# Gating h of the first MoE straight out of the PSUM banks it is computed in

## The chip, the cores and the metric

The program runs on one core of a Trainium2 chip. Its engines are TensorE (PE in the rows; PEld are its weight loads), VectorE (DVE), ScalarE (ACT), GpSimd (POOL) and SyncE (SP), each with its own queue that it works off strictly in order; they meet through semaphores. [...] The metric is the device time of one execution in microseconds, as the median of several. The profile is of one execution.

## The reference

```
X   = fft(fft(x, axis=1), axis=2).real          # x: 8 x 3072 x 256, fp32
h   = X @ w_in                                   # 24576 tokens, 256 -> 2048
g   = h * clip(h + 3, 0, 6) / 6
y   = g @ w_out                                  # 2048 -> 256
e   = argmax(y @ w_gate);  p = softmax(y @ w_gate)[e]       # one of 8 experts a token
out = p * relu(y @ w1[e]) @ w2[e]                # 256 -> 1024 -> 256; out: 24576 x 256
```

## The kernel before, in words

Every fp32 product is made of three TensorE products in the fp32r type (high part by high, high by low, low by high), so each operand of a matmul is kept as a high part (a ScalarE copy that rounds) and a low part (operand minus high part).

The first phase, some 2090 us of the span, does the transform and the first MoE. A *step* (`step(s)`, 384 of them) takes 512 tokens and 256 of the 2048 columns of h. Eight steps (`STEPS`) make a *chunk* of tokens, 48 steps a batch. One step consists of:

- `mm1`: 14 matmuls of 256 columns into a tile `ab` of two PSUM banks, A in the first and B in the second.
- `h_of`: ScalarE copies A to SBUF (tile `A`), and VectorE forms h for tokens k and for the mirrored tokens: `h[0] = A - B` and `h[1] = A + B`, each 128x512.
- the gates: `relu6` on ScalarE gives r = relu(h/6 + 1/2) for both halves; `gate_h` on VectorE puts min(r, 1)*h in r's place; ScalarE copies it to `gh` (the high part), and GpSimd subtracts, `gl = r - gh`.
- `mm2` of the step three before (`LAG`): 16 matmuls of 264 columns with `gh` and 8 with `gl` into four accumulator banks `acc`, over the eight steps of a chunk.

The tiles `ab` come from a pool of two (four banks); the four `acc` banks are the other half of PSUM. A piece of the transform (`fft_g0`, `fft_g12`: 13 to 28 matmuls, tiles `fe`, `fo`, `f`) takes a tile of the same pool of two; there is one piece in each chunk, at the step in which the accumulators of the chunk before are read out too. That step also begins the routing of the finished chunk (`routing`: small VectorE and GpSimd work, four indirect DMAs from GpSimd's queue), and its rank product rides in the free half of the transform's tile. In the other steps VectorE also folds the input of the next batch: one operation, now and then two, on the SBUF tiles `R` and `H` (516 or 774 elements a partition), after a step's gates.

In the kernel before the gates of step s are written in step s+1 and read h from an SBUF tile `h` (two buffers a half). The order on each engine is not the order of the code: a scheduler sorts the instructions by priority and by its own model of when a buffer is free, and the pools decide how many steps may be under way. An instruction marked `keep_in_program_order` is left where the code has it; that mark is on the folds, not on matmuls.

The second phase, some 1260 us, runs the experts on tiles of 512 or 256 routed tokens. No line of it changes.

Of the lines that matter:

```
BUFS = dict(h=2, r=4, gh=4, gl=4)                                    # before
ab_ps = ps1.enter_context(tc.tile_pool(name="ab_ps", bufs=2, space=PSUM))
```

Of the kernel before, what the change touches and what calls it, by code (L numbers as in the profile page):

```python
# [10 lines left out]
F32 = mybir.dt.float32  # L11
# [5 lines left out]
AF = mybir.ActivationFunctionType  # L17
# [9 lines left out]
GW = 264  # L27
# [16 lines left out]
EC = 5  # L44
EX = 6
RKW = 4
BUFS = dict(h=2, r=4, gh=4, gl=4)
EXTRA = 23
LATE = (0, 0, 1, 1, 2, 3, 3, 4, 5, 5, 6, 6, 7, 7, 8, 8, 8, 9)
RK = 2  # L50
# [24 lines left out]
def tile_fft_moe(ctx, tc, xr, xf, xcoef, w_in, w_out, w_gate, w1, w2, tabs, fm, misc, tri, sgn8, dstc, maskc, out):  # L75
# [24 lines left out]
    tiles, hold = {}, {}  # L100
# [21 lines left out]
    def wo(i, f):  # L122
        if (i, f // 8) not in WOh:
            WOh[i, f // 8] = pc.tile([P, 8, GW], F32R, tag=f"WO{i}{f // 8}", name=f"WO{i}{f // 8}")
        return WOh[i, f // 8][:, f % 8]
# [20 lines left out]
    dve, act, pool, pe, sp = nc.vector, nc.scalar, nc.gpsimd, nc.tensor, nc.sync  # L146
# [6 lines left out]
    def ab_tile(name):  # L153
        hold["last"] = t = ab_ps.tile([P, 2, 512], F32, tag="ab", name=name)
        return t


    def bank(name):
        if "hp" in hold:
            return hold["hp"].tile([P, 512], F32, tag="hp", name=name)  # L160
        return ab_tile(name)[:, 1]

    def mm_group(dst, terms):
        for n, (l, r) in enumerate(terms):
            pe.matmul(dst, l, r, start=(n == 0), stop=(n == len(terms) - 1))  # L165

    def pinned(i):
        if hold.get("fold"):
# [11 lines left out]
    def add(eng, o, a, b):  # L180
        pinned(eng.tensor_tensor(out=o, in0=a, in1=b, op=ALU.add))  # L181

    def sub(eng, o, a, b):
        i = eng.tensor_tensor(out=o, in0=a, in1=b, op=ALU.subtract)  # L184
        pinned(i)
        return i
# [79 lines left out]
    def xterm(b, c0, n):  # L266
        return [(XN[:, c0:c0 + P], sgn_of[b][:, 0:n])]

    def fft_g0(b, pq):
        def e_mm(st):  # L270
            ab = st["ab"] = ab_tile(f"fe{b}_0")
            mm_group(ab[:, 0, 0:258], fft_terms(SC0, 0, 0, "c", 0) + xterm(b, X_T0, 258))
            mm_group(ab[:, 1, 0:256], fft_terms(SC0, 1, 0, "c", 1))

        def e_ev(st):
            ab = st["ab"]
            v = lambda i: pq[:, i].rearrange("p (a c) -> p a c", a=2)
            act.activation(v(0), ab[:, :, 0:256], AF.Copy)
            dve.tensor_copy(pex[:, b:b + 1], ab[:, 0, 256:257])
            dve.tensor_tensor(out=v(1), in0=ab[:, :, 0:256], in1=v(0), op=ALU.subtract)  # L280

        def o_mm(st):
            ab = st["ab2"] = ab_tile(f"fo{b}_0")
            for i, n, c0 in ((0, 258, X_T0 + P), (1, 256, X_T1)):
                full = fft_terms(SS0, 1 - i, 0, "s", i) + xterm(b, c0, n)
                edge = fft_terms(SC0, i, P, "c", i, 1)
                for t, (l, r) in enumerate(full[:1] + edge + full[1:]):
                    rows = slice(0, 1 if 0 < t <= len(edge) else P)
                    pe.matmul(ab[rows, i, 0:n], l, r, start=t == 0, stop=t == len(full + edge) - 1)

        def o_ev(st):
            ab = st["ab2"]
            v = lambda i: pq[:, i].rearrange("p (a c) -> p a c", a=2)
            act.activation(v(2), ab[:, :, 0:256], AF.Copy)
            dve.tensor_copy(qex[:, b:b + 1], ab[:, 0, 256:257])
            dve.tensor_tensor(out=v(3), in0=ab[:, :, 0:256], in1=v(2), op=ALU.subtract)

        return [(e_mm, e_ev), (o_mm, o_ev)]
# [191 lines left out]
        for i in range(2):  # L490
            mm_group(ab[:, 1, i * 256:(i + 1) * 256], [(WB[a][:, f[i]], pq[:, 2 + c, c0:c0 + 256]) for a, c in PASS])

    def h_of(ab, h, s):
        A = pw.tile([P, 2, 256], F32, tag="Ac", bufs=AB, name=f"A{s}")
        v = [ab[:, n].rearrange("p (i n) -> p i n", i=2) for n in range(2)]
        act.activation(A, v[0], AF.Copy)  # L496
        sub(dve, h[0], A, v[1])
        add(dve, h[1], A, v[1])

    def relu6(r, h):  # L500
        act.activation(r, h, AF.Relu, bias=half, scale=1.0 / 6.0)  # L501
# [2 lines left out]
    def halves(tag, dt, s):  # L504
        return [pw.tile([P, 2, 256], dt, tag=tag, bufs=BUFS[tag], name=f"{tag}{s}_{n}") for n in range(2)]

    def gate_h(g, r, h):
        dve.scalar_tensor_tensor(out=g, in0=r, scalar=1.0, in1=h, op0=ALU.min, op1=ALU.mult)  # L508

    def mm2(acc, gh, gl, f0, first, last, mid=(), ntau=4):  # L510
        def one(i, t, g, w, st, sp_):
            lhs = g[t // 2][:, i, (t % 2) * P:(t % 2 + 1) * P]
            pe.matmul(acc[t][:, 0:GW], lhs, wo(w, f0 + i), start=st, stop=sp_)  # L513
        for i in range(2):
            for t in range(ntau):
                one(i, t, gh, 0, first and i == 0, False)
                one(i, t, gh, 1, False, False)
            if i == 0:
                for f in mid:
                    f()  # L520
        if last:
            for t in range(ntau):
                for i in range(2):
                    one(i, t, gl, 0, False, i == 1)
        else:
            for i in range(2):
                for t in range(ntau):
                    one(i, t, gl, 0, False, False)
# [78 lines left out]
    if True:  # L607
# [52 lines left out]
        NS = len(chunks) * STEPS  # L660
# [257 lines left out]
        def plan_early():  # L918
            e0 = 8 * (NCH - EC) + 18 + RKW - 3
            fill[e0].append(lambda: None)  # L920
            pfill[e0].append(early_mm)
            fill[e0].append(early_pick)
            fill[e0 + 4].append(lambda: (first_sets(), load_x(0), load_w(0), load_x(1)))
            for n in range(4):
                fill[e0 + 6 + EG * n].append(lambda n=n: in_order(prep_w(0, lambda n: dve)[n]))
            fill[e0 + 10 + EX].append(lambda: prep_x(0))

        def step(s):
            z = s - LAG
            if s < NS:  # L930
                b, g, c = chunks[s // STEPS]
                f0 = 2 * (s % STEPS)
                ab = ab_tile(f"ab{s}")
                mm1(ab, f0, gt[(b, g)], c * 256, q3[s // STEPS % 2])
            hold["ride"] = None
            for f in pfill.pop(s, []):
                f()
            hold["ride"] = None
            if 0 <= z < NS:
                k = z % STEPS  # L940
                if k == 0:
                    hold["acc"] = [ac_ps.tile([P, 512], F32, tag=f"acc{t}", name=f"acc{z}_{t}") for t in range(4)]
                mm2(hold["acc"], *hold.pop(("g", z)), 2 * k, k == 0, k == STEPS - 1, mfill.pop(s, []))
            for f in afill.pop(s, []):
                f()
            hold["ride"] = None
            if s < NS:
                h = hold["h", s] = halves("h", F32, s)
                h_of(ab, h, s)
            if 0 < s <= NS:  # L950
                h = hold.pop(("h", s - 1))
                r, gh, gl = halves("r", F32, s), halves("gh", F32R, s), halves("gl", F32R, s)
                g = r
                for n in range(2):
                    relu6(r[n], h[n])
                for n in range(2):
                    gate_h(g[n], r[n], h[n])
                for n in range(2):
                    act.activation(gh[n], g[n], AF.Copy)  # L959
                for n in range(2):  # L960
                    sub(pool, gl[n], g[n], gh[n])
                hold[("g", s - 1)] = (gh, gl)
            if 0 <= z < NS and z % STEPS == STEPS - 1:
                xo = pw.tile([P, 4, GW], F32, tag="xo", bufs=1, name=f"xo{z}")
                xp = pw.tile([P, 4, XW], I32, tag="xp", name=f"xp{z}")
                with tc.high_priority(offset=6):
                    evac(hold["acc"], xo)
                halve(xo, xp)
                ci = z // STEPS
                b, g, c = chunks[ci]  # L970
                plan_routing(routing(xo, xp, ci * 4, 4, 0 if (g == 0 and c == 0) else None, f"c{ci}",
                             RKW if ci < NCH - 2 else 3), s + 1)
            for f in fill.pop(s, []):
                f()
            if s % STEPS == QB and s + STEPS < NS:
                load_q3(s // STEPS + 1)

        x0 = (NB - 1) * 6 * STEPS + EXTRA
        fill[x0 - 1].append(lambda: plan_extra(x0))
        plan_early()  # L980
        for s in range(NS + LAG):
            step(s)
        ps1.close()
        h_ps = ctx.enter_context(tc.tile_pool(name="h_ps", bufs=4, space=PSUM, reuse_waits="tile"))
        o_ps = ctx.enter_context(tc.tile_pool(name="o_ps", bufs=4, space=PSUM, reuse_waits="tile"))
# [33 lines left out]
        ge = pw.tile([P, NTILE, NE + 1], F32, tag="xp", name="ge")  # L1019
        tt = pw.tile([P, NTILE, NE], F32, tag="r", bufs=BUFS["r"], name="tt")  # L1020
        dve.memset(ge[:, :, 0:1], 1.0)
# [94 lines left out]
        full = last  # L1116
# [3 lines left out]
        n = nc.values_load(nus[0:1, 0:1], min_val=0, max_val=NSMALL, skip_runtime_bounds_check_because=why)  # L1120
# [159 lines left out]
```

## Time and profile before

| | |
|---|---|
| median of 3 runs | 3349.0 us (3348.02 to 3355.43) |
| profiled execution | 3351.21 us, span 3349.4 us |
| busy share of the span | PE 94%, PEld 90%, DVE 68%, ACT 58%, POOL 68% |
| mean granted TensorE clock | 0.979 of full |
| first phase, 150 to 2090 us | 361 of the 384 steps, 5.37 us a step |

The median of the runs lies 2.2 us under the profiled execution, so its rows can be summed without a correction of more than that. In a timeline a row is a run of equal instructions: its start in us from the span's start, how long it lasted, the engine, the line, the tiles it writes and reads, how many instructions it holds, and, where the engine stood idle before it, for how long and what ended that. TensorE overlaps consecutive matmuls, and the modelled end of the last of a row reaches into the next; the distance between starts tells its pace. VectorE and ScalarE overlap a little too: the next instruction can begin some 0.09 us before the one ahead of it ends.

### The profile page before, as it was taken

The numbers are of one execution on the slowest core, as the hardware profiler recorded it, in microseconds if no ns is written. First come the engines' busy times: TensorE is split into PE (matmuls) and PEld (weight loads), VectorE is DVE, ScalarE is ACT, GpSimd is POOL, SyncE is SP. The second block draws the span as 40 slices with busy tenths as digits, with TensorE's granted clock in tenths as the row PEclk, the third lists the DMA queues.
The fourth block names the chain that finished last, engine by engine and source line by source line (L and its number), as shares of the span: only waits on it lengthen the run. The fifth ranks groups of instructions, "written<-read, shape, count | busy, mean of one in ns | idle before, by whom it ended". The sixth has DMA issues, their size and how long they took to land.

```text
span 3349.4 us, 62616 instructions
## 1 busy us (share of the span) xinstructions
PE 3133.1 (94%) x23482; PEld 3001.7 (90%) x23482; DVE 2277.1 (68%) x3699; ACT 1934.1 (58%) x3339; POOL 2267.7 (68%) x1784
## 2 busy tenths in 40 slices
PE   5899999999999999999899999999999999999998
PEld 5899999899899899899899999988888888898887
DVE  8878777777777777777777676755555555555553
ACT  3566666566666566666566666645454444544453
POOL 5567776776776777677777776766676666666664
PEclk8999999999999999999999999999999999999999
DMA  5100100100100110000000002065555555545560
GB/s 180 61 28 21 36 25 14 43 24 16 39 28 16 33 33 16 30 30 17 31 14 16 14 18 51 20 193 154 144 168 149 143 149 158 147 145 154 147 171 30
DMA packets 256195, 243.18 MB, mean 73 GB/s; under 512 B 157739, under 2 KB 219020, under 8 KB 255888
## 3 DMA queue, kind: packets, MB, share of 16 engines
q1 hardware_dynamic: 234640, 184.66, 19.7%
q0 software_dynamic: 21248, 54.48, 4.5%
q8 instruction: 187, 3.06, 0.4%
q14 instruction: 120, 0.98, 0.1%
HBM read 159.71 MB, written 54.04 MB: 64 GB/s over the span
## 4 chain that ended last, share of the span: by engine, by line
PE 45%; DVE 18%; ACT 17%; issue 9%; POOL 5%; SPq 0%; DMA 0%; ACTq 0%; POOLq 0%; DVEq 0%
PE op L165 16%; PE hp L165 15%; PE acc L513 8%; ACT gh L959 7%; ACT r L501 6%; PE ab L165 5%; DVE h L184 4%; POOL gl L184 3%; DVE r L508 2%; POOL xs_dram L149 2%; DVE R L189 2%; DVE R L181 2%; DVE H L181 1%; ACT xp L539 1%; ACT xo L532 1%
## 5 line engine op out<-in xcount | busy, mean ns | idle before, releaser
L184 POOL TENSOR_TENSOR gl<-r,gh 128x512 fp32r<-128x512 f32 x768 | 1109.6, 1464 | 468.1 <-ACT gh L959 372.7
L501 ACT ACTIVATE r<-h,half 128x512 f32<-128x512 f32 x768 | 546.4, 719 | 610.1 <-DVE h L184 386.0
L508 DVE SCALAR_TENSOR_TENSOR r<-r,h 128x512 f32<-128x512 f32 x768 | 625.1, 818 | 369.3 <-ACT r L501 368.2
L513 PE MATMUL acc<-WO,gh 128*128 128x264 f32 x6144 | 824.4, 287 | 3.4 <-ACT xo L532 3.4
L513 PEld LDWEIGHTS acc<-WO,gh 128*128 128x128 f32 x6144 | 786.2, 192 | 3.6 <-ACT xo L532 3.6
L165 PE MATMUL ab<-pq,WA 128*128 128x256 f32 x2304 | 398.8, 290 | 107.4 <-DVE h L181 68.4
L995 DVE SCALAR_TENSOR_TENSOR WB<-hp,WA 128x512 fp32r<-128x512 f32 (+1 forms) x472 | 278.5, 606 | 301.8 <-ACT WA L994 301.7
L959 ACT ACTIVATE gh<-r 128x512 fp32r<-128x512 f32 x768 | 451.1, 622 | 42.6 <-DVE r L508 13.6
L513 PE MATMUL acc<-WO,gl 128*128 128x264 f32 x3072 | 444.6, 286 | 2.7 <-POOL gl L184 1.8
L165 PEld LDWEIGHTS ab<-pq,WA 128*128 128x128 f32 x2304 | 333.6, 193 | 120.3 <-issue 87.3
L513 PEld LDWEIGHTS acc<-WO,gl 128*128 128x128 f32 x3072 | 404.6, 189 | 6.1 <-POOL gl L184 5.6
L994 ACT ACTIVATE WA<-hp 128x512 fp32r<-128x512 f32 (+1 forms) x472 | 240.9, 529 | 197.5 <-PE hp L165 194.3
L165 PE MATMUL ab<-pq,WB 128*128 128x256 f32 x2304 | 349.2, 289 | 0.0
L149 POOL DMA_INDIRECT out_dram<-yo,dst x200 | 217.3, 1086 | 155.9 <-DVE yo L1095 118.3
L165 PEld LDWEIGHTS ab<-pq,WB 128*128 128x128 f32 x2304 | 314.2, 197 | 0.0
L149 POOL DMA_INDIRECT xs_dram<-xp,pic x192 | 212.6, 1107 | 125.6 <-DVE pic L599 68.9
L165 PE MATMUL hp<-xTb,TB 128*128 128x512 f32 (+1 forms) x1344 | 277.8, 364 | 13.9 <-DVE WB L995 13.9
L165 PE MATMUL hp<-xTa,W1b 128*128 128x512 f32 (+1 forms) x1392 | 277.0, 358 | 2.2 <-DVE WB L995 2.2
L165 PEld LDWEIGHTS hp<-xTb,TB 128*128 128x128 f32 x1344 | 226.3, 188 | 58.1 <-DVE WB L995 15.5
L165 PE MATMUL op<-W2b,WA 128*128 128x256 f32 x1536 | 276.3, 282 | 0.0
L165 PEld LDWEIGHTS hp<-xTa,W1b 128*128 128x128 f32 x1392 | 228.8, 189 | 43.3 <-DVE WB L995 2.6
L184 DVE TENSOR_TENSOR h<-A,ab 128x512 f32<-128x512 f32 x384 | 259.4, 675 | 6.7 <-ACT A L496 6.1
(269 smaller groups left out, 5479.7 us busy)
## 6 DMA issues: line engine op xcount, KB each, us to landing
w1a<-in_w_dram SPq DMA_DIRECT2D x29, 1024.0 KB
w1b<-in_w_dram SPq DMA_DIRECT2D x29, 1024.0 KB
w2b<-in_w_dram SPq DMA_DIRECT2D x58, 512.0 KB
R<-in_xr_dram SPq DMA_DIRECT2D x32, 774.0 KB
w2a<-in_w_dram SPq DMA_DIRECT2D x29, 768.0 KB
w2d<-in_w_dram SPq DMA_DIRECT2D x28, 256.0 KB
q<-pq SPq DMA_DIRECT2D x288, 1.0 KB
raw<-in_w_in_dram SPq DMA_DIRECT2D x8, 512.0 KB
```

The source lines that it names most:

```text
L149: i = pool.indirect_dma_start(oob_is_err=False, **kw)
L165: pe.matmul(dst, l, r, start=(n == 0), stop=(n == len(terms) - 1))
L181: pinned(eng.tensor_tensor(out=o, in0=a, in1=b, op=ALU.add))
L184: i = eng.tensor_tensor(out=o, in0=a, in1=b, op=ALU.subtract)
L189: pinned(dve.scalar_tensor_tensor(out=o, in0=a, scalar=s, in1=b, op0=ALU.mult, op1=ALU.add))
L501: act.activation(r, h, AF.Relu, bias=half, scale=1.0 / 6.0)
L508: dve.scalar_tensor_tensor(out=g, in0=r, scalar=1.0, in1=h, op0=ALU.min, op1=ALU.mult)
L513: pe.matmul(acc[t][:, 0:GW], lhs, wo(w, f0 + i), start=st, stop=sp_)
L532: act.activation(xo[:, t, :], acc[t][:, 0:GW], AF.Copy)
L959: act.activation(gh[n], g[n], AF.Copy)
L994: act.activation(hi, ps, AF.Relu)
L995: dve.scalar_tensor_tensor(out=lo, in0=ps, scalar=0.0, in1=hi, op0=ALU.max, op1=ALU.subtract)
```

## The change

The tile `h` is gone. `h_of` writes A - B over A in the first bank and A + B over B in the second, and returns the two banks as h; `relu6` and `gate_h` read them there. The gates of step s are written in step s itself, so `gh` and `gl` carry its number (before, they carry the number of the step after). The bytes of `h` go to two more buffers of `gl`, six for four. All matmuls of the first phase now go through a small function that would keep them in program order where `hold["steps"]` is set; it is set to False before the loop and after it, so no matmul is kept, and the scheduler orders TensorE as it did.

```
-BUFS = dict(h=2, r=4, gh=4, gl=4)
+BUFS = dict(r=4, gh=4, gl=6)
...
+    def matmul(*a, **kw):
+        i = pe.matmul(*a, **kw)
+        if hold.get("steps"):
+            tc.keep_in_program_order(i)
...
-    def h_of(ab, h, s):
+    def h_of(ab, s):
         A = pw.tile([P, 2, 256], F32, tag="Ac", bufs=AB, name=f"A{s}")
-        v = [ab[:, n].rearrange("p (i n) -> p i n", i=2) for n in range(2)]
-        act.activation(A, v[0], AF.Copy)
-        sub(dve, h[0], A, v[1])
-        add(dve, h[1], A, v[1])
+        h = [ab[:, n].rearrange("p (i n) -> p i n", i=2) for n in range(2)]
+        act.activation(A, h[0], AF.Copy)
+        sub(dve, h[0], A, h[1])
+        add(dve, h[1], A, h[1])
+        return h
...
             if s < NS:
-                h = hold["h", s] = halves("h", F32, s)
-                h_of(ab, h, s)
-            if 0 < s <= NS:
-                h = hold.pop(("h", s - 1))
+                h = h_of(ab, s)
                 r, gh, gl = halves("r", F32, s), halves("gh", F32R, s), halves("gl", F32R, s)
-                g = r
                 for n in range(2):
                     relu6(r[n], h[n])
                 for n in range(2):
-                    gate_h(g[n], r[n], h[n])
+                    gate_h(r[n], r[n], h[n])
                 for n in range(2):
-                    act.activation(gh[n], g[n], AF.Copy)
+                    act.activation(gh[n], r[n], AF.Copy)
                 for n in range(2):
-                    sub(pool, gl[n], g[n], gh[n])
-                hold[("g", s - 1)] = (gh, gl)
+                    sub(pool, gl[n], r[n], gh[n])
+                hold["g", s] = gh, gl
...
+        hold["steps"] = False
         for s in range(NS + LAG):
             step(s)
+        hold["steps"] = False
```

In the three pairs below, names carry buffer numbers (the last number of a name is only the buffer's), and the words in brackets name the engines whose semaphores the instruction waits for.

VectorE in a plain step, before: h of step 102, its gates (r103 is the r of h102), a fold, and the next h.

```order
L184 TENSOR_TENSOR h102_0_8000<-A102_8002,ab102_7961 128x512 [waits DVE_49,Activation_49]
L181 TENSOR_TENSOR h102_1_8001<-A102_8002,ab102_7961 128x512 [waits DVE_49]
L508 SCALAR_TENSOR_TENSOR r103_0_8073<-r103_0_8073,h102_0_8000 128x512 [waits Activation_49]
L508 SCALAR_TENSOR_TENSOR r103_1_8074<-r103_1_8074,h102_1_8001 128x512 [waits Activation_49]
L181 TENSOR_TENSOR H3_0_6581<-H3_0_6581 128x258
L184 TENSOR_TENSOR h103_0_8067<-A103_8069,ab103_8028 128x512 [waits DVE_49,Activation_49]
```

VectorE at the same place of the changed kernel, step 103.

```order
L189 TENSOR_TENSOR ab103_7836<-A103_7875,ab103_7836 128x512 [waits Activation_49]
L186 TENSOR_TENSOR ab103_7836<-A103_7875,ab103_7836 128x512 [waits DVE_49]
L515 SCALAR_TENSOR_TENSOR r103_0_7879<-r103_0_7879,ab103_7836 128x512 [waits Activation_49]
L515 SCALAR_TENSOR_TENSOR r103_1_7880<-r103_1_7880,ab103_7836 128x512 [waits Pool_49]
L186 TENSOR_TENSOR H3_0_6429<-H3_0_6429 128x258
L189 TENSOR_TENSOR ab104_7896<-A104_7935,ab104_7896 128x512 [waits Activation_49]
```

The sequence is the same. The second of the two h instructions now waits for the first (it overwrites what the first one reads), and only the first of the gates waits for ScalarE.

ScalarE in the same plain step, before: A of step 102, the relu of its two halves, and the high parts of the gates of the step ahead of it.

```order
L496 ACTIVATE A102_8002<-ab102_7961 128x512 [waits PE_49]
L501 ACTIVATE r103_0_8073<-h102_0_8000,half_101 128x512 [waits DVE_49,Pool_49]
L959 ACTIVATE gh102_0_8008<-r102_0_8006 128x512 [waits PE_49]
L959 ACTIVATE gh102_1_8009<-r102_1_8007 128x512 [waits PE_49]
L501 ACTIVATE r103_1_8074<-h102_1_8001,half_101 128x512 [waits DVE_49,Pool_49]
L496 ACTIVATE A103_8069<-ab103_8028 128x512 [waits PE_49]
```

ScalarE in the changed kernel, step 103; gh102 are the high parts of step 102's gates.

```order
L502 ACTIVATE A103_7875<-ab103_7836 128x512 [waits PE_49]
L962 ACTIVATE gh102_0_7816<-r102_0_7814 128x512 [waits DVE_49,PE_49]
L962 ACTIVATE gh102_1_7817<-r102_1_7815 128x512 [waits DVE_49,PE_49]
L508 ACTIVATE r103_0_7879<-ab103_7836,half_101 128x512 [waits DVE_49,Pool_49]
L508 ACTIVATE r103_1_7880<-ab103_7836,half_101 128x512 [waits Pool_49]
L502 ACTIVATE A104_7935<-ab104_7896 128x512 [waits PE_49]
```

The pair of high parts has moved from between the two relus to ahead of both. One wait on VectorE stands ahead of both relus, and it is for the second of the h instructions.

TensorE behind a piece of the transform, before: the last matmul into its tile f2_1_0, then mm1 of step 99, then mm2 of step 96 (whose gates are gh97 and gl97 here), then mm1 of step 100.

```order
L165 MATMUL f2_1_0_7682<-rt_occ10_7383,onesb_58 128x32
L165 MATMUL ab99_7744<-pq2_0_6534,WA0_69 128x256 x2
...
L165 MATMUL ab99_7744<-pq2_0_6534,WB1_72 128x256
L513 MATMUL acc96_0_7759<-WO00_490,gh97_0_7625 128x264
...
L513 MATMUL acc96_3_7762<-WO00_490,gl97_1_7628 128x264
L165 MATMUL ab100_7817<-pq2_0_6534,WA0_69 128x256 x2
```

The same place in the changed kernel, where the gates of step 96 are gh96 and gl96.

```order
L164 MATMUL f2_1_0_7500<-rt_occ10_7209,onesb_58 128x32
L164 MATMUL acc96_0_7575<-WO00_500,gh96_0_7385 128x264
...
L164 MATMUL acc96_3_7578<-WO00_500,gl96_1_7388 128x264
L164 MATMUL ab99_7560<-pq2_0_6384,WA0_69 128x256 x2
...
L164 MATMUL ab99_7560<-pq2_0_6384,WB1_72 128x256
L164 MATMUL ab100_7631<-pq2_0_6384,WA0_69 128x256 x2
```

The 24 matmuls of mm2 of step 96 now stand ahead of mm1 of step 99, and mm1 of step 100 follows mm1 of step 99 directly. In plain steps TensorE's order is unchanged.

## Rows read from the trace of the kernel before

**Rows 1.** Windows: length; PE, PEld, DVE, ACT, POOL busy; granted clock, DMA share, GB/s.

```profile
150.00:2090.00 1940.00, 1812.16 (x14561) 1784.60 (x14562) 1479.24 (x2474) 1246.89 (x2296) 1383.11 (x1243) 0.98 0.08 26
```

**Rows 2.** Timeline of TensorE: mm1 and mm2 of plain steps, mm1 behind a transform.

```profile
1174.01 0.52 PE L165 MATMUL ab<-pq,WA 128*128 128x256 f32 x3
...
1175.65 2.10 PE L513 MATMUL acc<-WO,gh 128*128 128x264 f32 x16
...
1178.57 0.52 PE L165 MATMUL ab<-pq,WA 128*128 128x256 f32 x3
...
1192.45 0.59 PE L165 MATMUL ab<-pq,WA 128*128 128x256 f32 x3 [1.98 <-DVE h L181]
```

**Rows 3.** Waits from 150 to 2090 us: waiter, awaited; us in total, times, longest.

```profile
ACT r L501 <- POOL gl L184: 168.5, 62, 4.0
...
PE ab L165 <- DVE h L181: 65.9, 47, 2.5
...
ACT A L496 <- PE ab L165: 13.2, 18, 1.9
```

**Rows 4.** Timeline of all engines in a plain step without a fold.

```profile
1001.00 0.67 DVE L184 TENSOR_TENSOR h<-A,ab 128x512 f32<-128x512 f32 x1
1001.59 0.67 DVE L181 TENSOR_TENSOR h<-A,ab 128x512 f32<-128x512 f32 x1
1001.76 0.72 ACT L501 ACTIVATE r<-h,half 128x512 f32<-128x512 f32 x1 [1.29 <-DVE h L184]
1002.39 1.14 ACT L959 ACTIVATE gh<-r 128x512 fp32r<-128x512 f32 x2
1002.52 0.69 DVE L508 SCALAR_TENSOR_TENSOR r<-r,h 128x512 f32<-128x512 f32 x1 [0.25 <-ACT r L501]
1003.09 3.00 POOL L184 TENSOR_TENSOR gl<-r,gh 128x512 fp32r<-128x512 f32 x2 [0.86 <-ACT gh L959]
1003.43 0.71 ACT L501 ACTIVATE r<-h,half 128x512 f32<-128x512 f32 x1
...
1004.18 0.75 DVE L508 SCALAR_TENSOR_TENSOR r<-r,h 128x512 f32<-128x512 f32 x1 [0.96 <-ACT r L501]
1004.85 0.67 DVE L184 TENSOR_TENSOR h<-A,ab 128x512 f32<-128x512 f32 x1
```

**Rows 5.** Timeline: three folds of 774 elements, and GpSimd beside them.

```profile
1093.27 2.99 POOL L184 TENSOR_TENSOR gl<-r,gh 128x512 fp32r<-128x512 f32 x2 [2.83 <-ACT gh L959]
...
1095.04 2.04 DVE L189 SCALAR_TENSOR_TENSOR R<-R 128x774 f32<-128x774 f32 x1
...
1117.87 0.96 DVE L181 TENSOR_TENSOR R<-R 128x774 f32<-128x774 f32 x1
...
1124.10 2.05 DVE L189 SCALAR_TENSOR_TENSOR R<-R 128x774 f32<-128x774 f32 x1
1125.28 1.36 POOL L181 TENSOR_TENSOR H<-R 128x258 f32<-128x258 f32 x1
```

**Rows 6.** Groups by form, 150 to 2090 us, DVE: count; busy us, mean ns; idle before.

```profile
L508 DVE SCALAR_TENSOR_TENSOR r<-r,h 128x512 f32<-128x512 f32 x720 | 578.1, 807 | 357.6 <-ACT r L501 356.6
L184 DVE TENSOR_TENSOR h<-A,ab 128x512 f32<-128x512 f32 x361 | 243.8, 675 | 6.1 <-ACT A L496 5.7
...
L181 DVE TENSOR_TENSOR H<-H 128x516 f32<-128x516 f32 x28 | 41.3, 1475 | 2.8 <-POOL H L184 2.8
L181 DVE TENSOR_TENSOR R<-R 128x774 f32<-128x774 f32 x26 | 40.2, 1545 | 0.0
...
L189 DVE SCALAR_TENSOR_TENSOR R<-R 128x774 f32<-128x774 f32 x26 | 36.9, 1418 | 0.0
L189 DVE SCALAR_TENSOR_TENSOR H<-H 128x516 f32<-128x516 f32 x28 | 34.4, 1228 | 0.0
```

**Rows 7.** The same view of ScalarE: copies from SBUF and from PSUM.

```profile
L959 ACT ACTIVATE gh<-r 128x512 fp32r<-128x512 f32 x722 | 423.7, 622 | 35.7 <-DVE r L508 11.4 <-DVE pic L599 10.6 <-PE acc L513 6.9
L496 ACT ACTIVATE A<-ab 128x512 f32<-128x512 f32 x360 | 209.7, 582 | 13.2 <-PE ab L165 13.2
```

More of the change, by code (lines that the diff above doesn't have):

```diff
@@ L161, in bank @@
         return ab_tile(name)[:, 1]
+    def matmul(*a, **kw):
+        i = pe.matmul(*a, **kw)
+        if hold.get("steps"):
+            tc.keep_in_program_order(i)
     def mm_group(dst, terms):
         for n, (l, r) in enumerate(terms):
-            pe.matmul(dst, l, r, start=(n == 0), stop=(n == len(terms) - 1))
+            matmul(dst, l, r, start=(n == 0), stop=(n == len(terms) - 1))
     def pinned(i):
@@ L288, in o_mm @@
                     rows = slice(0, 1 if 0 < t <= len(edge) else P)
-                    pe.matmul(ab[rows, i, 0:n], l, r, start=t == 0, stop=t == len(full + edge) - 1)
+                    matmul(ab[rows, i, 0:n], l, r, start=t == 0, stop=t == len(full + edge) - 1)
         def o_ev(st):
@@ L512, in one @@
             lhs = g[t // 2][:, i, (t % 2) * P:(t % 2 + 1) * P]
-            pe.matmul(acc[t][:, 0:GW], lhs, wo(w, f0 + i), start=st, stop=sp_)
+            matmul(acc[t][:, 0:GW], lhs, wo(w, f0 + i), start=st, stop=sp_)
         for i in range(2):
```

## Prediction

> **What bounds the kernel now.** I read the windows first, by stage. The edit touches only the first phase, so its 1940 us are the place to look. [...] TensorE's own timeline comes next. A plain step begins every 4.56 us, and mm2 takes 2.92 us of it [rows 2]. 361 such steps are 1646 us; the transform's pieces and the gaps make the rest of the 1940, or 5.37 us a step. The gaps lie behind the transform, where mm1 stood still for 1.98 us until an h instruction freed its banks [rows 2], and 47 such waits are 66 us [rows 3].
>
> Who makes h late? The waits say that ScalarE waited only 13 us for mm1 to hand over A [rows 3], and the groups that VectorE waited 5.7 us for A [rows 6]: mm1's result was nearly always there first. VectorE's queue is what runs without slack, with ScalarE's relus inside its loop. Counted from the first h instruction of a step [rows 4]: second h at 0.59, first relu 0.76, first gate 1.52, second relu 2.43 (ScalarE does two high parts in between), second gate 3.18, next step's h at 3.85. To these 3.85 us come folds, transform read-outs and routing. So the time of phase one is mostly VectorE's loop plus its other work, and TensorE's 4.56 us is the floor under it. The reader should see in these rows that TensorE, the busiest engine, is not what decides the next microsecond.
>
> **What the change does to that loop.** TensorE's wrapper pins nothing, since its switch is False throughout; that part costs and gives nothing of itself. What the scheduler moves, it moves because banks come free later.
>
> *The loop.* From the program's waits: first h 0, its own end 0.67; the second h may start only then, plus 0.04 (the wait that a gate has behind a relu: 1001.76 + 0.72 to 1002.52 [rows 4]), at 0.71, and ends at 1.38. The relus wait for it: first at 1.48 (0.09 from h's end to the relu, same rows), second 0.63 later at 2.11, end at 2.83. The first gate at 2.87; gates follow each other as the h instructions do, by 0.60, so the second at 3.47, and the next step's h at 4.07. That is 4.07 against 3.85, 0.22 us longer in each of 361 steps: **+79 us**. ScalarE reads A out of PSUM in 582 ns and an SBUF tile in 622 [rows 7]; if the relus gain the same 40 ns, two of them give back 29 us. No row shows VectorE writing PSUM. Nearest are its h instruction (675 ns [rows 6]) and its fast gate (690 [rows 4]), so I take no difference; from below I bound it by the relus' 40 ns (-29 us for two), from above by ScalarE's slowest 512-wide operation, 720 ns, so +45 ns a write, +32 us.
>
> [...]
>
> *Gates beside gl.* A gate takes 807 ns on the mean and 0.69 or 0.75 in the sample step [rows 6, 4]; the rest is gates that ran while GpSimd read SBUF. The h instructions, which take one operand from PSUM, are 675 on the mean and never longer in the sample. The new gate is of that kind. Beyond the 0.72 that the loop above contains for old gates: 721 x 87 ns, **-63 us** (ends: 0 and -95, the latter against 675).
>
> *Folds beside gl.* A fold of 774 elements took 2.04 us when it began behind a pair of gl on GpSimd, and 0.96 when it didn't; and one that began first made GpSimd's next operation, of 258 elements, last 1.36 us [rows 5]. The pair of gl starts 2.09 us into the step and lasts 3.0, the fold begins at 3.85 [rows 4]: it begins inside the pair each time. In the change the high parts stand ahead of the relus. The first can start when its gate is done (2.87 + 0.68) and takes 0.61, so gl of this step begins near 4.3 and ends near 7.3, which is 3.2 into the next step. The fold begins at 4.07: after the old pair, and 0.2 us before the new one. So folds should run free. The rows of the four big forms hold (1475 + 1228 - 2 x 675) x 28 + (1545 + 1418 - 2 x 960) x 26 ns = 65 us above the free price [rows 6]. Behind the routing's DMAs GpSimd lags, and folds will still meet it there: I take **-50** (ends 0 and -65).
>
> *The wait for GpSimd.* Relus waited 168 us, 62 times, 2.7 us each, for gl to free r [rows 3]. gl now starts 1.6 us earlier (4.3 instead of 3.85 + 2.09 after its step's first h). That takes more than half of 2.7 us off: 62 x 1.6 = 99, of which part lay beside other work of VectorE: **-85** (ends 0 and -168).
>
> *The banks.* They come free at the end of the second gate, 3.47 + 0.68 = 4.15, instead of the second h's, 0.59 + 0.67 = 1.26: 2.89 us later. With two tiles, mm1 of step s+2 naturally starts 9.1 us after that of step s. mm1 takes 1.6 us of it, A 0.6, the loop 4.15: 2.7 us of slack are left, half of what there was. Behind each transform piece the scheduler now places the 2.92 us of mm2 ahead of the waiting mm1, which covers the later release there. What is late next is VectorE, which now starves for A in light steps: its loop of 4.07 is under TensorE's 4.56, and with less slack it can't work ahead. Half of the 361 steps at 0.49 us would be 88; I take **+45** (ends 0 and 88). Queued behind a waiting mm1 is mm2, whose operands are three steps old. The first 150 us, where other products compete for the two tiles, I give +5.
>
> Sum: 79 - 63 - 50 - 85 + 45 + 5 = **-69 us**. From the profiled execution's 3351.2 that is 3282; the median of the runs is 2.2 lower, so **3280 us**, 2.1% faster. Six buffers of gl are nothing here: gl waits for its reader little, and starts earlier anyway.
>
> **Rivals.** *The held bank decides.* If VectorE is more than 2.7 us behind at the step behind a read-out, each of the 47 waits for h grows by the 2.89 us of the later release: +136 us, and with VectorE then waiting for TensorE, of the gains only the gates' -63 counts: 3349 + 136 - 63 = 3422. For it: those waits are there already, and VectorE works at its limit. Against it: mm2 moved ahead is as long as the delay, but only behind a transform piece.
>
> *The fold loses its 0.2 us race.* Then folds keep their price, GpSimd stays late and half of its gain goes: 79 - 63 - 0 - 42 + 45 + 5 = +24 at worst, and about nothing where the relus read PSUM faster: 3349, no change.
>
> *TensorE's floor.* All folds and waits for GpSimd go and VectorE doesn't starve: 79 - 63 - 65 - 168 is more than TensorE's 128 us of gaps allow; nine tenths of them gone is -115: 3234.
>
> **Chances.** My forecast 0.56, with its own range 3245 to 3335; the floor 0.13; no change 0.08; the held bank 0.23. The outer ranges: at the floor with the lower clock level gone too some 3215; half of the held bank's chance lies below 3410. So 3215 to 3410 holds eight in ten. 0.2% is 6.7 us, what a measurement of this kernel can tell from none. Faster: 0.56 + 0.13 and a little of the no-change case, 0.70; within it 0.07; slower 0.23.
>
> **What would show it.** Right: steps of VectorE of about 4.07 us without a fold; gates near 0.68 us with no long ones; folds of 774 near 0.96; relus waiting for gl under 80 us; fewer and shorter gaps of TensorE behind the transform. Wrong: mm1 waiting for the second gate (L515) for far more than 66 us, or folds still near 2 us on the mean. The second phase should last the same 1259 us.

## The result: 2.3% faster

The changed kernel takes 3272.6 us (median of 4 runs, 3270.4 to 3277.3); the kernel before takes 3349.8 us beside it. The ratio is 0.9772, with a 95% interval of 0.9759 to 0.9785: 77 us less, against 69 forecast. The profiled execution has a span of 3272.1 us.

The last matmul of mm2 ends at 2162 us before and at 2088 us after, so 74 of the 77 us came out of the first phase, which ends there and not at the 2090 us that were taken for its end; the rest lasts 1187 us before and 1184 after. The windows from 150 us to that point, first of the kernel before, then of the changed one (columns as in [rows 1]):

```profile
150.00:2163.00 2013.00, 1881.94 (x15120) 1853.60 (x15121) 1536.55 (x2565) 1297.32 (x2382) 1438.45 (x1291) 0.98 0.08 26
```

```profile
150.00:2089.00 1939.00, 1869.00 (x15190) 1840.32 (x15190) 1391.68 (x2571) 1318.77 (x2390) 1306.12 (x1300) 0.99 0.09 27
```

TensorE's gaps fell from 131 us (2013 - 1882) to 70, and its own time by 13 us with the granted clock from 0.98 to 0.99. VectorE works 145 us less and GpSimd 132 us less, on nearly the same work.

Which gaps went? The group of mm1's first matmuls, before and after, in the same windows (busy, mean, then the idle time before them and what ended it):

```profile
L165 PE MATMUL ab<-pq,WA 128*128 128x256 f32 x2232 | 383.6, 288 | 107.0 <-DVE h L181 68.4 <-DVE rt_kc L585 24.2 <-DVE rt_sc L587 7.1
L164 PE MATMUL ab<-pq,WA 128*128 128x256 f32 x2244 | 384.1, 287 | 64.6 <-DVE r L515 61.7 <-DVE WO L183 0.6 <-DVE rt_kc L592 0.6
```

The wait for h before (68 us) and for gates after (62 us) is nearly the same. What went are mm1's waits for VectorE's routing work (`rt_kc`, `rt_sc`, `rt_ixc`: 35 us before, 1 after) and the waits of the transform's own matmuls for VectorE (19 us before, 2 after).

A plain step of the changed kernel, VectorE and ScalarE, to hold against [rows 4] (timeline; in brackets the idle time before and what ended it):

```profile
1206.52 0.69 DVE L189 TENSOR_TENSOR ab<-A,ab 128x512 f32<-128x512 f32 x1
1207.24 0.69 DVE L186 TENSOR_TENSOR ab<-A,ab 128x512 f32<-128x512 f32 x1
1208.03 1.27 ACT L508 ACTIVATE r<-ab,half 128x512 f32<-128x512 f32 x2 [1.03 <-DVE ab L186]
1209.27 0.60 ACT L502 ACTIVATE A<-ab 128x512 f32<-128x512 f32 x1
1209.33 1.28 DVE L515 SCALAR_TENSOR_TENSOR r<-r,ab 128x512 f32<-128x512 f32 x2 [1.39 <-ACT r L508]
1210.53 0.69 DVE L189 TENSOR_TENSOR ab<-A,ab 128x512 f32<-128x512 f32 x1
```

Counted from the first h instruction: second h 0.72, relus 1.51, gates 2.81, next step's h 4.01. VectorE stands still for 1.39 us of it, between A + B and its first gate. A step with a fold, same view:

```profile
1129.78 0.69 DVE L189 TENSOR_TENSOR ab<-A,ab 128x512 f32<-128x512 f32 x1
...
1133.69 1.15 ACT L962 ACTIVATE gh<-r 128x512 fp32r<-128x512 f32 x2 [0.65 <-PE acc L164]
1133.79 0.69 DVE L186 TENSOR_TENSOR H<-H 128x516 f32<-128x516 f32 x1
1134.40 0.69 DVE L189 TENSOR_TENSOR ab<-A,ab 128x512 f32<-128x512 f32 x1
1134.40 2.53 POOL L189 TENSOR_TENSOR gl<-r,gh 128x512 fp32r<-128x512 f32 x2 [2.04 <-ACT gh L962]
```

This fold, of 516 elements, begins 4.01 us into the step, lasts 0.69 us, and is all but over when the pair of gl begins at 4.62. The pair takes 2.53 us where it took 3.00 [rows 4]. The groups of VectorE by form and the waits, 150 to 2089 us, against [rows 3, 6]:

```profile
L515 DVE SCALAR_TENSOR_TENSOR r<-r,ab 128x512 f32<-128x512 f32 x750 | 481.5, 684 | 453.4 <-ACT r L508 445.5 <-issue 7.2
L186 DVE TENSOR_TENSOR ab<-A,ab 128x512 f32<-128x512 f32 x374 | 259.9, 695 | 11.3
...
L194 DVE SCALAR_TENSOR_TENSOR R<-R 128x774 f32<-128x774 f32 x26 | 28.2, 1083 | 0.0
L186 DVE TENSOR_TENSOR R<-R 128x774 f32<-128x774 f32 x26 | 27.0, 1037 | 0.0
L194 DVE SCALAR_TENSOR_TENSOR H<-H 128x516 f32<-128x516 f32 x28 | 25.0, 893 | 0.0
...
L186 DVE TENSOR_TENSOR H<-H 128x516 f32<-128x516 f32 x28 | 21.1, 753 | 2.5 <-POOL H L189 2.5
```

```profile
ACT A L502 <- PE ab L164: 130.9, 171, 2.4
...
PE ab L164 <- DVE r L515: 61.7, 60, 2.4
...
DVE ab L189 <- ACT A L502: 20.9, 26, 2.0
...
ACT r L508 <- POOL gl L189: 5.7, 11, 0.7
```

Gates take 684 ns for 807; the four fold forms lie 0.3 to 0.7 us lower (of two further forms, of 516 elements of `R`, one falls from 1233 to 746 ns and one stays, 1187 and 1226); the relus wait 6 us for gl where they waited 168. And ScalarE now waits 131 us for mm1 where it waited 13: in plain steps it is ready before TensorE has A. VectorE's own waits for the relus did not fall, they grew from 364 to 445 us (before, in the window to 2163 us, and after):

```profile
DVE r L508 <- ACT r L501: 364.2, 519, 3.1
DVE r L515 <- ACT r L508: 445.5, 312, 3.4
```

TensorE behind a transform piece, against the last row of [rows 2]: mm2 stands ahead of mm1, and mm1 waits 0.53 us.

```profile
1110.04 0.18 PE L164 MATMUL f<-rt_occ,onesb 128*128 128x32 bf16 x1
1110.07 2.20 PE L164 MATMUL acc<-WO,gh 128*128 128x264 f32 x16
1112.11 1.12 PE L164 MATMUL acc<-WO,gl 128*128 128x264 f32 x8
1113.76 0.59 PE L164 MATMUL ab<-pq,WA 128*128 128x256 f32 x3 [0.53 <-DVE r L515]
```

### The profile page after: what moved, and what is told of

It is laid out like the page before. It is cut to its first block, busy times and chain, and to the rows that moved or that the text cites. A ratio compares the mean times of both kernels' runs of the same rounds, so it can differ in the third digit from the quotient of the medians.

```text
span 3272.1 us, 61901 instructions
## 1 busy us (share of the span) xinstructions
PE 3116.5 (95%) x23482; PEld 2983.7 (91%) x23482; DVE 2117.7 (65%) x3699; ACT 1952.4 (60%) x3339; POOL 2123.1 (65%) x1784
## 4 chain that ended last, share of the span: by engine, by line
PE 61%; DVE 22%; ACT 10%; issue 3%; POOL 2%; DMA 1%; SPq 0%; ACTq 0%; DVEq 0%; POOLq 0%
PE op L164 16%; PE acc L164 16%; PE hp L164 15%; PE ab L164 11%; DVE r L515 6%; ACT r L508 5%; DVE ab L186 3%; DVE ab L189 3%; ACT xp L546 1%; ACT gh L962 1%; DVE H L194 1%; ACT xo L539 1%; PE wi L164 1%; DVE H L186 1%; DVE xTa L189 1%
## 5 line engine op out<-in xcount | busy, mean ns | idle before, releaser
L189 POOL TENSOR_TENSOR gl<-r,gh 128x512 fp32r<-128x512 f32 x768 | 1018.7, 1349 | 541.4 <-ACT gh L962 536.7
L515 DVE SCALAR_TENSOR_TENSOR r<-r,ab 128x512 f32<-128x512 f32 x768 | 493.0, 683 | 460.8 <-ACT r L508 452.9
L508 ACT ACTIVATE r<-ab,half 128x512 f32<-128x512 f32 x768 | 486.2, 684 | 241.0 <-DVE ab L186 219.5
L164 PE MATMUL ab<-pq,WB 128*128 128x256 f32 x2304 | 342.3, 285 | 0.0
L502 ACT ACTIVATE A<-ab 128x512 f32<-128x512 f32 x384 | 230.1, 599 | 158.7 <-PE ab L164 138.6
L189 DVE TENSOR_TENSOR ab<-A,ab 128x512 f32<-128x512 f32 x384 | 264.7, 689 | 32.8 <-ACT A L502 25.3
L186 DVE TENSOR_TENSOR ab<-A,ab 128x512 f32<-128x512 f32 x384 | 266.8, 695 | 11.5
```

Source lines behind the costliest of these rows:

```text
L164: i = pe.matmul(*a, **kw)
L502: act.activation(A, h[0], AF.Copy)
```

## The experiments

The question was which of the things that the one edit does at once are worth what: the step in which the gates are written, ScalarE's order, the place of h, the six buffers, TensorE's order. Eleven kernels ran. "Slower" and "faster" with a ratio are against the kernel before; its median stayed at 3348 to 3349 us.

**1. h back in SBUF, gates still at once.**

```
-BUFS = dict(r=4, gh=4, gl=6)
+BUFS = dict(h=2, r=4, gh=4, gl=4)
...
-        h = [ab[:, n].rearrange("p (i n) -> p i n", i=2) for n in range(2)]
...
+        v = [ab[:, n].rearrange("p (i n) -> p i n", i=2) for n in range(2)]
+        h = halves("h", F32, s)
...
+        sub(dve, h[0], A, v[1])
+        add(dve, h[1], A, v[1])
```

> The changed kernel with h back in an SBUF tile (two buffers) and four buffers of gl; the gates stay written in the step that makes their h. The scheduler then gives ScalarE the order that the kernel before had: A, first relu, two high parts of the step before, second relu. Theory (the gain came from the order on ScalarE, which starts GpSimd's low parts about 1.6 us earlier in the step, so that folds and gates no longer run beside them and the relus no longer wait for them): nothing of that is here, gates about 0.80 us on the mean, folds of 774 elements about 1.5 us, relus waiting 150 us or more for gl, time 3345 us (3330 to 3355). Rival (writing the gates at once is what helps, wherever h lies): 3275 us. Rival (holding the PSUM banks cost something, and without it the same edit is faster still): under 3260 us.

Measured: 3427.8 us, ratio 1.0239 (1.0225 to 1.0253), slower than any case expected. From the groups and waits of its first phase, up to 2010 us (it ends at 2241):

```profile
L516 DVE SCALAR_TENSOR_TENSOR r<-r,h 128x512 f32<-128x512 f32 x660 | 532.9, 814 | 399.2 <-ACT r L509 398.0 <-issue 0.5
...
L186 DVE TENSOR_TENSOR R<-R 128x774 f32<-128x774 f32 x26 | 51.0, 1963 | 0.0
...
L194 DVE SCALAR_TENSOR_TENSOR R<-R 128x774 f32<-128x774 f32 x26 | 44.4, 1709 | 0.0
```

```profile
ACT r L509 <- POOL gl L189: 147.8, 65, 3.8
PE ab L164 <- DVE h L186: 142.5, 87, 3.9
```

With the high parts between the relus again, all three prices are back: long gates, long folds, the wait for gl. Folds are longer still than before (1963 and 1709 ns for 1545 and 1418), and mm1 waits 142 us for h where it waited 66; that wait is as much as the 78 us by which it is slower than the kernel before. Why h is so late with nearly the same order on ScalarE stays open. So writing the gates at once is no gain by itself. The rival on held banks finds no support here, but ScalarE's order changed along with the banks, so this run alone does not settle it.

**2. h in SBUF, ScalarE's order fixed by hand.** As run 1, and the two high parts of the step before are written ahead of the relus and kept there:

```
+            if 0 < s <= NS:
+                r = hold.pop(("r", s - 1))
...
+                    tc.keep_in_program_order(act.activation(gh[n], r[n], AF.Copy))
...
+                    tc.keep_in_program_order(act.activation(r[n], h[n], AF.Relu, bias=half, scale=1.0 / 6.0))
```

> h in SBUF with two buffers and four buffers of gl, as in the kernel before, but ScalarE's order is fixed by hand: A of a step, then the two high parts of the step before, then both relus. No gate reads PSUM and no bank is held longer. Theory (that order is what the change was worth): gates at 0.70 us on the mean or less, relus waiting for gl under 40 us, folds of 774 near 1.05 us, VectorE's plain step about 2.8 us where it does not wait for TensorE; time 3260 us (3235 to 3285), so all of the gain or more. Rival (the gates are cheap because their second operand is in PSUM): gates stay near 0.80 us and the time near 3330 us. Rival (two more buffers of gl are what took the relus' wait away): relus wait 150 us or more, time 3320 to 3345 us.

Measured: 3269.0 us, ratio 0.9762 (0.9748 to 0.9775): the time of the changed kernel, with h in SBUF. Against run 1 the order on ScalarE, with GpSimd's gl behind it, is worth 159 us. The time is in the theory's range, but its means were wrong: the relus wait 126 us for gl (under 40 expected), folds of 774 take 1459 and 1311 ns (1050), and the gates, up to 2010 us:

```profile
L516 DVE SCALAR_TENSOR_TENSOR r<-r,h 128x512 f32<-128x512 f32 x720 | 747.0, 1061 | 223.8 <-ACT r L968 223.0 <-issue 0.7
```

```profile
1129.01 2.65 DVE L516 SCALAR_TENSOR_TENSOR r<-r,h 128x512 f32<-128x512 f32 x2 [0.26 <-ACT r L968]
1129.36 6.15 POOL L189 TENSOR_TENSOR gl<-r,gh 128x512 fp32r<-128x512 f32 x4
```

The gates run beside gl now, and a pair of them takes 2.65 us instead of 1.28. Same time, by another road: VectorE waits 226 us for the relus over the first phase instead of 445, and pays that back in dearer gates.

**3. Four buffers of gl.** `gl=6` back to `gl=4`, nothing else.

> The changed kernel with four buffers of gl in place of six, nothing else. Prediction's step (six buffers are nothing): within 0.2% of the changed kernel, 3266 to 3280 us. Rival (a low part now made early lies for three steps until its mm2, so four halves, two steps, make GpSimd wait for the mm2 of two steps ago, which frees r late again): GpSimd waiting over 300 us for acc matmuls, relus waiting 100 us or more for gl, time 3310 to 3345 us.

Measured: 3269.0 us (3265.4 to 3270.1), 0.1% from the changed kernel. GpSimd does wait 321 us for mm2, as the rival said, but the relus feel 20 us of it. Six buffers are nothing in this kernel.

**4. One-bank tiles.**

```
-    ab_ps = ps1.enter_context(tc.tile_pool(name="ab_ps", bufs=2, space=PSUM))
+    ab_ps = ps1.enter_context(tc.tile_pool(name="ab_ps", bufs=4, space=PSUM))
...
-        hold["last"] = t = ab_ps.tile([P, 2, 512], F32, tag="ab", name=name)
+        hold["last"] = t = Pair([ab_ps.tile([P, 512], F32, tag="ab", name=f"{name}_{n}") for n in range(2)])
```

> The changed kernel with the two banks of a step as two tiles of one bank each (four buffers), so that the first relu waits for A - B alone and the first gate for the first relu alone; in the changed kernel they wait for A + B and for the second relu, because both banks are one tile. VectorE's plain step then takes about 2.8 us where nothing is late, in place of 4.0. Theory (VectorE's loop, with its other work, is still what makes mm1 wait behind the transform): mm1 waits for gates under 20 us in place of 62, TensorE's clock above 0.985, time 3235 us (3215 to 3255), although the scheduler puts the high parts behind the relus again and some folds may meet gl. Rival (a plain step of 4.0 us is under TensorE's 4.56 us already, so a shorter loop buys nothing): 3266 to 3280 us. Rival (folds and gates beside gl decide): folds of 774 near 1.5 us again and the time 3300 us or more.

Measured: 3260.6 us, ratio 0.9736 (0.9723 to 0.9749): 12 us better than the changed kernel, between the theory and its rivals. Operations that read both banks at once are written twice here, once a bank. mm1 still waits 62 us for gates, where the theory said under 20. The scheduler put the high parts behind the relus, gl starts where the folds do, and folds cost more than in the kernel before (1545 and 1418 ns):

```profile
L194 DVE TENSOR_TENSOR R<-R 128x774 f32<-128x774 f32 x26 | 46.5, 1789 | 0.0
...
L202 DVE SCALAR_TENSOR_TENSOR R<-R 128x774 f32<-128x774 f32 x26 | 41.8, 1608 | 0.0
```

**5. The kernel before with its folds ahead of the gates.**

```
-                    fill[u0 + at[n + 3] + 1].append(lambda f=f: in_order(f))
+                    ffill[u0 + at[n + 3] + 1].append(lambda f=f: in_order(f))
...
-                fill[u0 + n].append(lambda f=f: in_order(f))
+                ffill[u0 + n].append(lambda f=f: in_order(f))
...
                 h_of(ab, h, s)
+            for f in ffill.pop(s, []):
+                f()
```

The first pair of lines moves the folds that GpSimd does, the second those of VectorE; runs 7, 9 and 11 move VectorE's alone.

> The kernel before with one edit: the folds are written between A + B and the gates of a step, so that VectorE does them while it waits for the relus, before GpSimd's pair of gl starts. Gates, h and buffers as before. Theory (a fold pays about 1 us where it runs beside gl, and that was a term of the change's gain): folds of 774 fall from 1.48 to about 1.05 us on the mean and hide in VectorE's two waits for the relus; a step with a fold then takes little more than 3.85 us in place of 5.8; time 3290 us (3265 to 3315). Rival (what the fold cost is given back by the gate behind it, or TensorE's waits lie elsewhere): 3335 us or more.

Measured: 3244.2 us, ratio 0.9694 (0.9681 to 0.9707), better than the change itself. Folds of 774 take 1501 and 1030 ns, less of a fall than expected, and gates grow from 815 to 864 ns over the whole first phase, part of what the rival said. But VectorE's waits for the relus fall from 364 to 259 us: the folds now stand in them. That is as much as the whole gain of 104 us.

**6. One-bank tiles and ScalarE's order of run 2.** The edits of runs 4 and 2, with h in PSUM.

> One-bank tiles as in the run with the split, h in PSUM, and ScalarE's order fixed by hand as in the run with h in SBUF: A, the two high parts of the step before, both relus. It differs from that run (3269 us, gates 1.06 us on the mean) in where h lies alone. Theory (beside a running gl a VectorE operation on two SBUF operands waits for GpSimd, one with an operand in PSUM does not): gates 0.69 us on the mean with gl at the same place, VectorE busy some 250 us less, time 3230 us (3210 to 3250). Rival (VectorE has slack in a loop of 2.8 us, so cheaper gates buy nothing; what is left is set elsewhere, by routing and the banks): gates 0.69 us too, but time 3255 to 3270 us.

Measured: 3164.6 us (3160.9 to 3172.4), ratio 0.9457 (0.9444 to 0.9470), beyond the theory's range, and the fastest kernel of the study. Its gates up to 1950 us, two rows in which they run beside gl, and the window to the end of its first phase:

```profile
L529 DVE SCALAR_TENSOR_TENSOR r<-r,ab 128x512 f32<-128x512 f32 x736 | 481.9, 683 | 360.0 <-ACT r L981 353.8 <-issue 1.1
...
1145.55 2.54 POOL L197 TENSOR_TENSOR gl<-r,gh 128x512 fp32r<-128x512 f32 x2 [2.02 <-ACT gh L974]
1146.60 1.29 DVE L529 SCALAR_TENSOR_TENSOR r<-r,ab 128x512 f32<-128x512 f32 x2 [1.87 <-ACT r L981]
```

```profile
150.00:1976.00 1826.00, 1822.30 (x15072) 1809.62 (x15072) 1378.85 (x2561) 1288.45 (x2378) 1277.67 (x1286) 1.00 0.09 28
```

TensorE is busy 1822 of 1826 us at a granted clock of 1.00: this phase is at TensorE's floor. Against run 2 h has moved to one-bank tiles in PSUM, and gl has six buffers for four, so it does not differ in the place of h alone: a gate costs 683 ns instead of 1061, and the time falls by 104 us. The price of the gate is shown by the rows. How much of the 104 us the buffers give is not: in run 3 they were nothing, but in run 2 GpSimd waits 129 us for mm2, here hardly at all, and run 2 with six of them was not run.

**7. Runs 4 and 5 together.**

> One-bank tiles as in the run with the split (3261 us, folds of 774 elements at 1.70 us on the mean, beside gl), and the folds written between A + B and the gates of a step, where the pair of gl of the step before has not begun or is nearly done. Theory (the split's gain is partly eaten by its folds, 24 us a hundred of them): folds of 774 near 1.1 us, VectorE busy about 80 us less in the first phase, time 3235 us (3220 to 3250). Rival (VectorE is no longer what the time hangs on): the same folds, and 3255 to 3265 us.

Measured: 3195.2 us, ratio 0.9547 (0.9534 to 0.9560), below the theory's range. Folds of 774 fall to 1080 and 1221 ns, and the time by 65 us, more than twice what was expected: VectorE still was what the time hung on.

**8. TensorE kept in the order of the code.** `hold["steps"] = True` ahead of the loop.

> The changed kernel with the switch of the new matmul function set to True for the whole first phase: the scheduler no longer orders TensorE, mm1 of a step stands ahead of mm2 as the code has it, behind a transform too. Theory of the prediction (the later release of the banks is covered only since the scheduler puts a 2.92 us mm2 ahead of the mm1 that waits): mm1 waits for the second gate about 45 times 2.5 us longer, time 3340 us (3310 to 3380). Rival (the order of TensorE matters little, VectorE's work sets when the banks come free): 3265 to 3285 us.

Measured: 3341.6 us (11 runs), ratio 0.9976 (0.9967 to 0.9985): nearly all of the gain is gone, and the time is where the prediction's theory put it. mm1 follows the transform and waits 1.77 us, where it waited 0.53 us behind mm2 in the changed kernel's row:

```profile
1187.54 0.18 PE L164 MATMUL f<-rt_occ,onesb 128*128 128x32 bf16 x1
1189.49 0.59 PE L164 MATMUL ab<-pq,WA 128*128 128x256 f32 x3 [1.77 <-DVE r L515]
```

Over the first phase (150 to 2157 us) mm1's waits for gates sum to 99 us, 62 in the changed kernel: 37 more, a third of the 112 that were expected. In all TensorE's gaps grew by 45 us, and its busy time by 23 (1892 us for 1869) at a granted clock of 0.97 against 0.99, so a part is time at a lower clock: behind the 1.77 us wait the last six matmuls of mm1 take 1.28 us from the first start to the start of mm2, in the next step 0.70 us. That the time hit 3340 is in part luck. The switch holds every matmul of the phase in place, not only those behind a transform.

**9. The changed kernel with its folds ahead of the gates.** The edit of run 5 on the changed kernel, for VectorE's folds alone.

> The changed kernel with the folds written between A + B and the gates, where VectorE waits 1.4 us for the relus. In the changed kernel a fold runs behind the gates, lengthens the 4.0 us step to 4.6 to 5.0 us, and is mostly free of gl already (1.06 us on the mean for 774 elements). Theory (VectorE's loop is what is left to gain): the fold hides in that wait but meets the end of the pair of gl of the step before, 1.4 us in place of 1.06; time 3235 us (3215 to 3255). Rival (the banks, held until the second gate, decide behind the transform, and folds in other steps don't matter): mm1 waits 60 us as before and the time is 3260 us or more.

Measured: 3189.4 us, ratio 0.9524 (0.9511 to 0.9537), 83 us below the changed kernel and below the theory's range. mm1 waits 12.5 us for gates (150 to 2003 us) where it waited 62, with the banks held until the second gate as before. So the rival falls: the banks' release was late because VectorE was.

**10. Gates written a step later, h in PSUM.**

> The changed kernel with the gates written one step later, as the kernel before had them, but h still in the banks: a bank is held until the gates that follow the next step's h. Theory of the rival in the prediction (the held bank decides): mm1 of step s+2 then waits for gates that stand behind h of step s+1, so that mm1, A, h and two gates, 1.65 + 0.6 + 1.4 + 1.3 us and some 0.3 between them, stand in one row for every step: 5.3 us a step in place of 4.56, time near 3500 us, mm1 waiting for gates over 200 us. If the bank's hold is not what counts even then: under 3360 us.

Measured: 3246.5 us, ratio 0.9690 (0.9675 to 0.9705). This did not test what it was for. In plain steps the scheduler moved the gates up to where they had been, ahead of the next step's h:

```profile
1130.82 1.28 DVE L515 SCALAR_TENSOR_TENSOR r<-r,ab 128x512 f32<-128x512 f32 x2 [1.39 <-ACT r L508]
1132.02 0.69 DVE L189 TENSOR_TENSOR ab<-A,ab 128x512 f32<-128x512 f32 x1
1132.74 0.69 DVE L186 TENSOR_TENSOR ab<-A,ab 128x512 f32<-128x512 f32 x1
```

Steps round a change of chunk differ, and the time is 26 us below the changed kernel's; which of the moves there did it stays open, and so does what a bank that is really held longer would cost.

**11. Runs 6 and 5 together.**

> One-bank tiles, the two high parts of the step before ahead of both relus on ScalarE, and the folds between A + B and the gates: the three edits that helped each by itself, h in PSUM. Theory (the run with the first two, 3165 us, stands at TensorE's floor: TensorE waits 16 us in all in its first phase): little is left, 3155 to 3165 us. Rival (folds still take 1.0 to 1.4 us at the end of a step beside gl and hold up h): 3145 us or less.

Measured: 3171.6 us, ratio 0.9468 (0.9454 to 0.9482): nothing over run 6, if anything a little slower, and 6 us above the theory's range. TensorE's gaps are 11 us in its first phase (4 in run 6): at TensorE's floor a cheaper fold has nothing to give.

## Why the prediction was right, step by step

- *The loop*: 4.01 us in the trace against 4.07 worked out, with every part within 0.1 us. Right, at 58 us (0.16 us in 361 steps) for the 79 forecast. Its price is the relu that waits for both h and the gate that waits for both relus, because two banks are one tile; run 6, which splits the tile, shows what can be had there.
- *Gates*: 684 ns with no long ones, forecast 0.68. The reason given (an operand from PSUM keeps GpSimd out of the gate's way) was an argument then; runs 2 and 6 show the times, 1061 against 683 ns with gates beside gl. So r and h from SBUF pay (1061 ns), r from SBUF and h from PSUM don't (683), nor does `A` with a bank (675 ns in the kernel before, 689 and 695 in the changed one). By what mechanism GpSimd lengthens them was not shown.
- *Folds*: the four big forms hold 52 us less ((1475 + 1228 - 893 - 753) x 28 + (1545 + 1418 - 1083 - 1037) x 26 ns), forecast 50. But the lead of the fold was 0.6 us and not 0.2: gl starts at 4.62, not near 4.3, since the high parts wait for mm2 (0.65 us in the row above). That wait was missing from the sum, and it helped.
- *The relus' wait for gl*: 168 us to 6; forecast "under 80", and 85 us of gain. The wait went as forecast, and twice as far; how little of it shows in the time is told below the list.
- *Banks and starving*: mm1's waits for the gates are no longer than those for h were (62 us for 66), so the rival of the held bank, at 0.23 the largest, was too dear by far. That TensorE's new order, with mm2 ahead of mm1 behind a transform, covers the later release is shown by run 8: without it, 69 us go. VectorE waited 21 us for A (6 before): 15 us for the 45 forecast.
- *TensorE's gaps*: the prediction named only the 66 us of waits for h, half of the 128 (1940 - 1812 us [rows 1]). By the rows above that half stayed, and the other half, waits for the routing's and the transform's work on VectorE, is what went. What a lower clock costs, which the range's 3215 counts on, no run shows by itself; the trace of the kernel before has a granted clock of 0.50 from 1193.0 to 1196.0 us, behind the 1.98 us wait [rows 2], and 0.98 on the mean [rows 1], and run 6, with 1.00 over its first phase, took 3164.6 us.
- *Six buffers* are nothing (run 3). *The first 150 us*: TensorE did 664 matmuls there for 731; at 0.12 us each (38 in 4.56 us) some 8 us were lost, forecast 5.
- *Not in the sum*: relus from PSUM take 684 ns against 718 from SBUF (run 2), 34 ns, near the 40 allowed for. VectorE's writes into PSUM take 689 and 695 ns for 675, within the bounds. The gate from PSUM (683 to 684 ns) is no longer than the free one from SBUF (690 [rows 4]).

So the sum came out right, 69 for 77, with the mechanisms of gates, folds and loop as described, but its closeness is in part luck. With the measured sizes in their places its terms would give 58 - 63 - 52 - 163 + 15 + 8 = -197 us, more than TensorE's gaps held. The term that fits least is the relus' wait for gl: ScalarE stopped waiting there, but VectorE's waits for the relus grew from 364 to 445 us, so the 163 us don't show in the time as such, and the judgement of 85 for them happened to fit. VectorE's own account of the phase is 145 us less work and 71 us more idle time, which makes the 74 us. What took the rest back can't be read off one by one; the relus still wait 218 us for A + B. What the prediction did not see is how much was left: with finer tiles and a fixed order on ScalarE, 108 us more (run 6).

## What to carry to other kernels

Where VectorE and GpSimd do elementwise work at the same time, ask where each operand lies: a VectorE operation with both operands in SBUF grew from 690 [rows 4] to 1061 ns (run 2) beside GpSimd here, and one with an operand in PSUM did not grow (683 ns, run 6). When a tile spans two banks, look at who waits for the half that he doesn't read: one-bank tiles with the same bytes were worth 108 us here, together with an order on ScalarE that the program kept itself (12 us without it). Work that has no deadline belongs into a wait that the engine has in every step, not behind the last instruction on which other engines depend: 104 us in run 5, 83 in run 9, and nothing in run 11, where TensorE was the floor already.

## What was not expected of the hardware

Two gates on SBUF operands beside four gl took 2.65 us, and gl itself 1.49 us on the mean instead of 1.33 (run 2 against run 6): both sides pay. A fold of 774 elements took 0.96 us or 2.05 us by what GpSimd did [rows 5]; a low part of only 258 elements, for the transform, took 3.53 us in the changed kernel while GpSimd did a pair of gl and its own folds:

```profile
1198.14 2.54 POOL L189 TENSOR_TENSOR gl<-r,gh 128x512 fp32r<-128x512 f32 x2
1198.73 3.53 DVE L183 SCALAR_TENSOR_TENSOR SC0s<-H,SC0s 128x258 fp32r<-128x258 f32 x1
1200.65 0.64 POOL L186 TENSOR_TENSOR H<-R 128x258 f32<-128x258 f32 x1
1201.24 1.27 POOL L189 TENSOR_TENSOR H<-R 128x258 f32<-128x258 f32 x2
```
